# Scan and gated network on one core: ten pairs' B and C turned by a transposing DMA instead of by TensorE and VectorE

## The chip, the core and the metric

The kernel runs on one core of a Trainium2 chip. Its engines run side by side, each through its own list of instructions in the listed order: TensorE (PE in the profile; PEld for its weight loads), VectorE (DVE), ScalarE (ACT), GpSimd (POOL), and SyncE (SP), which only issues transfers. An instruction waits on semaphores for what other engines or transfers give it, and everything listed behind it on that engine waits too. Transfers run on 16 DMA engines; SP's and ScalarE's are put on hardware queues, GpSimd's on a software queue. The metric is device time in microseconds, a median over runs.

## The reference

A scan over chunks (batch 4, 8 heads, 768 tokens, head size 32, state size 16) feeds a gated network (3072 tokens, 256 to 1536 to 256).

```
cum  = cumsum(log(clip(a, 1e-6, 1)))            # within a chunk of 32 tokens
M    = (C_i . B_j) * exp(cum_i - cum_j), j <= i
y    = M @ x + exp(cum_i) * (C_i . state)
state = exp(sum) * state + sum_j exp(cum_end - cum_j) B_j x_j
...
x2   = y as (tokens, heads * head size)
out  = (max(x2 @ w_gate, 0) * (x2 @ w_val)) @ w_out
```

Inputs and output are float32.

## The kernel before, in words

**Scan.** Instead of chunks of 32 tokens the kernel uses tiles of 128 tokens with all 8 heads, two tiles to a *pair*: 12 pairs of 256 tokens, three to a batch. The decay is moved into the factors: with P the running product of a, B is scaled by 1/P and C by P, so C_i . B_j of the scaled values already holds exp(cum_i - cum_j). `cp` holds P; the matmuls `dec` and `wdec` spread it over tokens by partition, and `scaleBC` (from `dec`) or `wf` (from `wdec`) hold P and 1/P. For pair p:

- `load`, `load_wide`, `load_seq`: raw x, B, C from memory, on SP's queue.
- `scale_bc` on GpSimd multiplies B and C by their factors and rounds them to bf16; `cast_x` rounds x.
- B and C must then be turned: tokens on partitions become heads times state on partitions. `turn` does this on PE (matmuls `tp`, `tpc` against the identity), and `tevac` evacuates to `CT` and to `BT`, the latter twice with a mask `tmask`, so that of a 32-row group only one head's 16 rows are not zero.
- `G`: 16 small matmuls of BT and CT into four PSUM banks; `gevac` applies the causal mask on VectorE (`maskUT`) or copies on ScalarE and masks on GpSimd (`causal`), into `gs`.
- `astep` and `sevac` carry the state of a batch's earlier tiles (`A_ps`, `Sm`); `inter` multiplies it by CT, `Dm` multiplies gs by x; both add into the PSUM bank `y`, which `yevac` copies to `yT`.

Three forms stand in the kernel before. Pairs 0 to 3 (p < `NWIDE`) are loaded in two-token runs, so a partition holds two neighbouring tokens; the pair must be sorted back for the state, which the matmuls `bp` against `order` do (`sort_b`). Pairs 4 and 5 are loaded in token order. Batches 2 and 3 (pairs 6 to 11, p >= `NRUN`) read B and C a second time as sequences (`load_seq`), compute decays a second time in that layout (`seq_scan` to `seq_inverse`), scale them on GpSimd (`seq_scale`), turn them with 32 by 32 transposes on VectorE (`seq_turn`) and mask them there (`seq_part`); their carried state comes from `arun`, which runs the small matmuls of one or two earlier tiles into `XY`, with the masks `smasks`.

**Network.** Tokens go in 6 blocks of 512. `gv` (all 512 tokens, one slice of 128 of the 1536) and `gvp` (256 tokens, two slices) make gate and value on PE, ReLU on ScalarE, product on VectorE into `h`; `outs` multiplies h by `wo`, evacuates and stores.

**Order.** The program is one list written by hand: the last part of the function calls these pieces in the order in which each engine is to run them, so that the network's matmuls of earlier blocks stand between a pair's steps. `in_order` makes each engine keep that order. A `hold` argument puts a one-element write on VectorE ahead of a load, so that the load is issued no sooner than VectorE gets there. Weights are loaded by GpSimd's queue (`weights`, `weights_out`).

## Time and profile before

| what | value |
|---|---|
| median of 3 runs | 124.62 us (124.45 to 124.63) |
| profiled execution | 124.8 us, of it 123.0 span |
| granted TensorE clock | 1.0 |
| GpSimd busy | 40% of the span |
| read from memory, written | 11.94 MB, 3.15 MB |

The span is the time from the first to the last instruction of the program; the execution's time has 1.8 us around it. In timeline rows the first number is the start and the second the length, in microseconds from the span's start. In groups, after xcount come busy time, mean ns of one, and the idle time before them with what ended it. A DMA view names the queues (q1 is SP's, q10 ScalarE's, q0 GpSimd's) with packets, megabytes and their share of the 16 engines' time; its issue rows end with the microseconds from issue to landing. A matmul's length includes its way through the array, so starts, not lengths, show how densely PE runs.

### The profile page before, as it was taken

Reading aid. Unit: us, or ns where it says so; the run is one execution under the profiler, and the core shown is the slowest. Engines: PE = TensorE matmul, PEld = TensorE weight load, DVE = VectorE, ACT = ScalarE, POOL = GpSimd, SP = SyncE. Lnnn points to the kernel's source line nnn. Section 1 sums busy time; section 2 is a strip of 40 time slices with the busy share of each in tenths; the row PEclk is TensorE's granted clock in tenths of the full one; section 3 lists DMA queues with packets and bytes.
Section 4 is the critical chain, followed back from the end, with each engine's and each line's share of the span. In section 5 each row is a group of like instructions: output and inputs, shape, how many; then the busy total and the mean of one; then the engine's idle time right before and its main releaser. Section 6 shows DMA issues by size and latency. Waiting matters only on the chain.

```text
span 123.0 us, 3313 instructions
## 1 busy us (share of the span) xinstructions
PE 118.3 (96%) x1251; PEld 81.1 (66%) x1257; DVE 92.1 (75%) x196; ACT 74.6 (61%) x148; POOL 49.7 (40%) x102
## 2 busy tenths in 40 slices
PE   6999999999999999999999999999999999999990
PEld 4678795578888989744478644588544587444780
DVE  2786898889999859879995889981898770678420
ACT  4376668888764461767663776746676644767310
POOL 7989741885745676477330640030700030000000
PEclk9999999999999999999999999999999999999999
DMA  2999999999989979969921282003200003100022
GB/s 61 201 193 209 168 167 190 130 102 174 162 101 278 140 137 191 199 201 211 132 24 62 83 137 22 5 0 106 70 3 0 0 5 128 43 0 0 0 91 85
DMA packets 63568, 12.95 MB, mean 105 GB/s; under 512 B 55168, under 2 KB 63552, under 8 KB 63552
## 3 DMA queue, kind: packets, MB, share of 16 engines
q1 hardware_dynamic: 54160, 9.47, 42.9%
q0 software_dynamic: 4272, 2.36, 14.6%
q10 hardware_dynamic: 5120, 0.90, 3.9%
q8 instruction: 10, 0.16, 0.5%
q14 instruction: 6, 0.05, 0.1%
HBM read 11.94 MB, written 3.15 MB: 123 GB/s over the span
## 4 chain that ended last, share of the span: by engine, by line
PE 95%; DVE 1%; issue 0%; ACTq 0%; ACT 0%; DVEq 0%
PE o L760 25%; PE val L707 20%; PE gate L704 18%; PE gate L734 7%; PE val L734 6%; PE w L189 4%; PE y L670 3%; PE g L544 3%; PE y L660 2%; PE A_ps L586 1%; PE tp L486 1%; PE wdec L232 1%; PE dec L279 1%; PE o L796 1%; PE bp L463 1%; PE fdec L247 0%
## 5 line engine op out<-in xcount | busy, mean ns | idle before, releaser
L719 DVE TENSOR_TENSOR h<-r,val 128x512 bf16<-128x512 bf16 x54 | 35.9, 685 | 10.2 <-ACT r L715 9.6
L715 ACT ACTIVATE r<-gate 128x512 bf16<-128x512 f32 x54 | 32.2, 598 | 12.2 <-PE gate L704 11.7
L707 PE MATMUL val<-yT,wv 128*128 128x512 bf16 x108 | 32.1, 379 | 0.3
L760 PE MATMUL o<-wo,h 128*128 128x256 bf16 x276 | 32.3, 273 | 0.0
L704 PE MATMUL gate<-yT,wg 128*128 128x512 bf16 x102 | 30.8, 379 | 0.0
L552 POOL TENSOR_SCALAR_AFFINE_SELECT gs<-gs 128x512 bf16<-128x512 bf16 (+1 forms) x26 | 13.6, 547 | 41.6 <-ACT gs L569 41.6
L760 PEld LDWEIGHTS <-h 128*128 128x128 bf16 x276 | 26.2, 98 | 4.0
L576 DVE TENSOR_TENSOR gs<-g,maskUT 128x512 bf16<-128x512 f32 (+1 forms) x32 | 17.6, 601 | 7.1 <-PE g L544 4.0
L707 PEld LDWEIGHTS <-wv 128*128 128x128 bf16 x108 | 10.6, 98 | 12.7
L704 PEld LDWEIGHTS <-wg 128*128 128x128 bf16 x108 | 10.4, 98 | 11.1
L569 ACT CAST gs<-g 128x512 bf16<-128x512 f32 (+1 forms) x26 | 11.8, 512 | 2.9 <-PE g L544 2.9
L742 ACT ACTIVATE r<-gate 128x512 bf16<-128x512 f32 x18 | 10.6, 604 | 2.7 <-PE gate L734 2.3
L749 DVE TENSOR_TENSOR h<-r,val 128x512 bf16<-128x512 bf16 x18 | 11.8, 678 | 0.3 <-ACT r L742 0.2
L734 PE MATMUL gate<-yT,wg 128*128 128x256 bf16 x72 | 10.8, 273 | 0.0
L734 PE MATMUL val<-yT,wv 128*128 128x256 bf16 x72 | 10.8, 273 | 0.0
L779 ACT COPY ob<-o 128x512 f32<-128x512 f32 x6 | 3.5, 586 | 8.6 <-PE o L760 8.6
L774 ACT COPY ob<-o 128x256 f32<-128x256 f32 x10 | 3.7, 373 | 7.3 <-PE o L760 6.8
L734 PEld LDWEIGHTS <-wv 128*128 128x128 bf16 x72 | 7.0, 98 | 0.9
L692 ACT CAST yT<-y 128x512 bf16<-128x512 f32 x10 | 5.9, 586 | 2.4 <-PE y L670 2.3
L734 PEld LDWEIGHTS <-wg 128*128 128x128 bf16 x72 | 6.7, 98 | 0.9
L189 PE MATMUL w<-warm 128*128 128x256 bf16 x27 | 5.9, 380 | 1.2 <-DVE tmask L159 1.2
L452 POOL CAST xb<-xr 128x512 bf16<-128x512 f32 x10 | 6.1, 612 | 1.0 <-DMA xr<-in_x_dram 1.0
(124 smaller groups left out, 123.2 us busy)
## 6 DMA issues: line engine op xcount, KB each, us to landing
xr<-in_x_dram SPq DMA_DIRECT2D x24, 128.0 KB, 3.7
out_dram<-ob SPq DMA_DIRECT2D x6, 256.0 KB, 2.6
out_dram<-ob SPq DMA_DIRECT2D x9, 128.0 KB, 1.8
wo<-in_moe_w_out_dram POOLq DMA_DIRECT2D x1, 768.0 KB, 8.9
seqB<-in_B_dram SPq DMA_DIRECT2D x2, 384.0 KB, 3.7
seqC<-in_C_dram SPq DMA_DIRECT2D x2, 384.0 KB, 4.2
br<-in_B_dram SPq DMA_DIRECT2D x12, 64.0 KB, 3.2
wg<-in_moe_w_gate_dram POOLq DMA_DIRECT2D x3, 128.0 KB, 4.3
```

What stands on the lines that cost most here:

```text
L189: nc.tensor.matmul(out=w[:, 0:cols], lhsT=warm[:, 0:128], rhs=warm[:, 0:cols], start=True, stop=True)
L552: nc.gpsimd.affine_select(out=dst, in_=dst, pattern=[[0, n], [1, 128]], compare_op=ALU.is_ge, fill=0.0, base=0, channel_multiplier=-1)
L569: nc.scalar.copy(out=d[:, q, h], in_=g[q][:, h])
L576: nc.vector.tensor_tensor(out=d[:, q, h], in0=g[q][:, h], in1=m[:, h], op=ALU.mult)
L704: nc.tensor.matmul(out=g, lhsT=wg[:, k, fs], rhs=yT[:, k, tk], start=(k == 0), stop=(k == 1))
L707: nc.tensor.matmul(out=v, lhsT=wv[:, k, fs], rhs=yT[:, k, tk], start=(k == 0), stop=(k == 1))
L715: nc.scalar.activation(r, g, AF.Relu)
L719: nc.vector.tensor_tensor(out=fst[b][:, f], in0=r, in1=v, op=ALU.mult)
L734: nc.tensor.matmul(out=o[:, j], lhsT=w[:, k, fs], rhs=yT[:, k, tk], start=(k == 0), stop=(k == 1), skip_group_check=True)
L742: nc.scalar.activation(r, g, AF.Relu)
L749: nc.vector.tensor_tensor(out=fst[b][:, f:f + 2, u * 256:(u + 1) * 256], in0=r, in1=v, op=ALU.mult)
L760: nc.tensor.matmul(out=o[:, ts % 2], lhsT=fst[b][:, f, ts * 128:(ts + 1) * 128], rhs=wo[:, f], start=(f == 0), stop=(f == NF - 1), skip_gr ...
```

## The change

Pairs 0 and 1 stay as they are (`NWIDE` is 2). Pairs 2 to 11 all take one form:

- `load_bc` loads C in two-token runs (`cr`) and B in token order (`br`, two loads of 64 KB).
- The decays come from `dec` alone: `decay_evac` copies them on ScalarE, in two parts, to `cN`; `inverse` makes `iN` = 1/cN on VectorE; `decay_sort` brings cN into two-token order, `wC`, by four transfers on SP's queue, from SBUF to SBUF.
- `scale_bc` on GpSimd writes B, scaled by iN, into the diagonal blocks (`diag`) of one of four tiles `pads` whose rest was set to zero once: for each of the two token tiles one slice with the even heads and one with the odd ones, 128 columns each. C, scaled by wC, goes into two more slices. For pairs 6 to 11 a fourth multiply writes B without padding, for `arun`.
- `dturn` turns the six slices with one transposing DMA on SP's queue into `TT` (128 x 6 x 128, bf16). G reads TT: the zeros of the padding take the place of the masked second copy of BT.
- The state step of pairs 2 to 5 uses the padded slices: two matmuls of 128 columns, even and odd heads, in place of one of 256; no sorting matmuls.
- C's two-token order makes the columns of G, gs and y run over the even, then the odd tokens: the causal masks have that order (`maskW`, a longer pattern in `causal`), and `yevac` writes every other column of yT.
- The second decays, sequence loads, scalings, turns and masks of batches 2 and 3 go, and so do `turn`, `sort_b`, `tevac` and `wdec` for pairs 2 to 5.
- x of pair 1 is loaded behind the first scaling multiply of pair 0 on VectorE; the holds on pair 3's loads go; B and C of pair 3 are loaded ahead of x of pair 2.

On SP, from the start of its list to the loads of pair 3's x. Before (xr is raw x, bcr raw B and C):

```order
L138 DMA a_sb<-in_a_dram 64x384
L95 DMA xr<-in_x_dram 128x8x32 x4
L83 DMA bcr<-in_B_dram 128x8x32
L83 DMA bcr<-in_C_dram 128x8x32
L95 DMA xr<-in_x_dram 128x8x32 x2
L83 DMA bcr<-in_B_dram 128x8x32
L83 DMA bcr<-in_C_dram 128x8x32
L95 DMA xr<-in_x_dram 128x8x32 x2
```

and now:

```order
L119 DMA a_sb<-in_a_dram 64x384
L95 DMA xr<-in_x_dram 128x8x32 x4
L105 DMA cr<-in_C_dram 128x8x32
L109 DMA br<-in_B_dram 128x8x16 x2
L288 DMA wC<-cN 64x80 x4
L105 DMA cr<-in_C_dram 128x8x32
L109 DMA br<-in_B_dram 128x8x16 x2
L95 DMA xr<-in_x_dram 128x8x32 x2
L342 DMA_TRANSPOSE TT<-pad_119 128x6x128
L342 DMA_TRANSPOSE TT<-pad_120 128x6x128
L95 DMA xr<-in_x_dram 128x8x32 x2
```

The transposes of pairs 2 and 3 stand behind the loads of B and C of both pairs and x of pair 2, and the loads of pair 3's x behind the transposes.

On GpSimd, from pair 1's last weights to the load of wo. Before (bs is a pair's scaled B and C, xb rounded x):

```order
L202 DMA wv<-in_moe_w_val_dram 128x2x384
L433 TENSOR_TENSOR bs<-bcr,wf_437 128x512
L452 CAST xb<-xr 128x512
L552 AFFINE_SELECT gs<-gs 128x512 x2
L552 AFFINE_SELECT gs<-gs 128x256
L433 TENSOR_TENSOR bs<-bcr,wf_437 128x512
L206 DMA wo<-in_moe_w_out_dram 128x12x256
```

and now:

```order
L189 DMA wv<-in_moe_w_val_dram 128x2x384
L315 TENSOR_TENSOR pad_119<-br,iN 128x4x2x16 x2
L319 TENSOR_TENSOR pad_119<-cr,wC 128x256
L315 TENSOR_TENSOR pad_120<-br,iN 128x4x2x16 x2
L319 TENSOR_TENSOR pad_120<-cr,wC 128x256
L367 CAST xb<-xr 128x512
L835 MEMSET pad_117 128x512
L835 MEMSET pad_118 128x512
L449 AFFINE_SELECT gs<-gs 128x512 x2
L449 AFFINE_SELECT gs<-gs 128x256
L193 DMA wo<-in_moe_w_out_dram 128x12x256
```

Both pairs are scaled, two tiles cleared and pair 2's x rounded ahead of pair 2's masks and the load of wo.

On PE, ahead of G of pair 2, between groups 6 and 7 of block 0. Before (bs is scaled B and C, ident the identity):

```order
L707 MATMUL val<-yT,wv 128x512
L486 LDWEIGHTS bs
L486 MATMUL tp<-ident,bs 128x128
L486 LDWEIGHTS bs
L486 MATMUL tp<-ident,bs 128x128
L486 LDWEIGHTS bs
L486 MATMUL tpc<-ident,bs 128x128
L486 LDWEIGHTS bs
L486 MATMUL tpc<-ident,bs 128x128
L463 LDWEIGHTS order
L463 MATMUL bp<-bs,order 128x128
```

and now, at the end of group 7:

```order
L620 MATMUL val<-yT,wv 128x512
L620 LDWEIGHTS wv
L620 MATMUL val<-yT,wv 128x512
L438 LDWEIGHTS TT
L438 MATMUL g_527<-TT 128x128
```

Group 7 follows group 6 without the transposes and sorting matmuls, and G reads TT.

The core of the diff:

```diff
-    NWIDE = 4
+    NWIDE = 2
...
+    def load_bc(p, q=nc.sync, hold=False):
+        br = raw.tile([128, 2, NH, N], FP32, tag="br", name="br")
+        cr = raw.tile([128, NH, 2, N], FP32, tag="cr", name="cr")
+        if hold:
+            nc.vector.memset(cr[0:1, 0, 0, 0:1], 0.0)
+        sl = slice(c0 * 128, (c0 + 2) * 128)
+        q.dma_start(out=cr.rearrange("p h r n -> p h (r n)"),
+                    in_=C[b, :, sl, :].rearrange("h (p r) n -> p h (r n)", r=2))
         for i in range(2):
             sl = slice((c0 + i) * 128, (c0 + i + 1) * 128)
+            q.dma_start(out=br[:, i], in_=B[b, :, sl, :].rearrange("h s n -> s h n"))
...
+    def decay_evac(d, part):
+        by = cN.rearrange("p i (b t) h -> p i t b h", t=PPB)
+        if not part:
+            nc.scalar.copy(out=by[:, 0, 0:2], in_=d[:, 0:HC:2, 0])
+            nc.scalar.copy(out=by[:, 1, 1:3], in_=d[:, 0:HC:2, 1])
+        else:
+            nc.scalar.copy(out=by[:, 1, 0], in_=d[:, 1, 0])
+            nc.scalar.copy(out=by[:, 0, 2], in_=d[:, 1, 1])
+    def decay_sort():
+        for i in range(2):
+            for r in range(2):
+                nc.sync.dma_start(out=wC[64 * i:64 * i + 64, r, NWIDE:NPAIR],
+                                  in_=cN[r:128:2, i, NWIDE:NPAIR])
+    def inverse(p0, p1):
+        nc.vector.reciprocal(iN[:, :, p0:p1], cN[:, :, p0:p1])
...
+        if p >= NWIDE:
+            s["pad"] = t = pads[p % NPAD]
+            for i in range(2):
                 eng.tensor_tensor(
+                    out=diag(t, 2 * i), in0=s["br"][:, i].rearrange("s (q t) n -> s q t n", t=2),
+                    in1=iN[:, i, p].rearrange("s (q t) -> s q t", t=2).to_broadcast(
+                        [128, 4, 2, N]), op=ALU.mult)
+            eng.tensor_tensor(
+                out=t[:, 4:6].rearrange("s r (h n) -> s r h n", n=N),
+                in0=s["cr"].rearrange("s h r n -> s r h n"),
+                in1=wC[:, :, p].to_broadcast([128, 2, NH, N]), op=ALU.mult)
...
+    def dturn(p):
+        s = st[p]
+        s["TT"] = att.tile([128, 6, 128], BF16, tag="TT", name="TT")
+        nc.sync.dma_start_transpose(out=s["TT"], in_=s["pad"].rearrange("s k m -> s (k m)"))
...
     first_scale(0, fB, bs0[:, 0:2])
+    load_x(1, True)
     first_scale(1, dC, bs0[:, 2:4])
...
-    load_wide(2, nc.sync, True)
-    load_x(2)
+    load_bc(2, nc.sync, True)
...
-    decay_evac(dall)
+    decay_evac(dall, 0)
     split_y(0)
+    decay_evac(dall, 1)
+    decay_sort()
+    load_bc(3)
+    load_x(2)
...
-    d2 = wide_decay([2, 3], later)
-    wide_factors([2, 3], d2)
     gvp_mul(*u4)
-    load_wide(3, nc.sync, True)
+    scale_bc(2, nc.gpsimd)
+    dturn(2)
+    scale_bc(3, nc.gpsimd)
+    dturn(3)
     load_x(3)
...
-    u = gv_relu(*gv(0, 6, False))
-    turn(2, True)
-    sort_b(2, False)
-    tevac(2, nc.vector, nc.scalar)
-    gv_mul(*u)
-    sort_evac(2)
+    gv(0, 6)
     gv(0, 7)
     G(2)
...
+        if more:
+            scale(Q, nc.gpsimd, nc.gpsimd)
+        if P + 3 < NPAIR:
+            load(P + 3)
+        if more:
+            dturn(Q)
+        if P + 4 < NPAIR:
+            load(P + 4)
...
             if f == 4 and R < NPAIR:
                 scale(R, nc.gpsimd, nc.gpsimd)
+                dturn(R)
```

350 lines of the change are left out of this document (101 added, 249 removed).

## The prediction

> **What bounds the kernel now.** I read the page first: engines, slices, chain of waits.
>
> ```profile
> span 123.0 us, 3313 instructions
> PE 118.3 (96%) x1251; PEld 81.1 (66%) x1257; DVE 92.1 (75%) x196; ACT 74.6 (61%) x148; POOL 49.7 (40%) x102
> DMA  2999999999989979969921282003200003100022
> PE 95%; DVE 1%; issue 0%; ACTq 0%; ACT 0%; DVEq 0%
> ```
>
> TensorE (PE) is busy for 96% of the span and makes 95% of the chain. A microsecond off PE's list is a microsecond off the time; one off VectorE, ScalarE or GpSimd is worth nothing by itself. The DMA engines are the second resource: a slice is 3.1 us, and from the second slice to about 58 us they are nearly full. A step that comes to hang on a DMA in that stretch waits behind a backlog.
>
> **What leaves PE's list.** The timeline of PE around the operations that go:
>
> ```profile
> 15.13 0.27 PE L586 MATMUL A_ps<-xb,bx 128*128 128x256 bf16 x1
> 15.33 0.68 PE L232 MATMUL wdec<-pick,cp 64*64 64x8 f32 x16
> 15.94 0.61 PE L734 MATMUL gate<-yT,wg 128*128 128x256 bf16 x4
> ...
> 19.43 0.28 PE L486 MATMUL tp<-ident,bs 128*128 128x128 bf16 x2
> 19.55 0.28 PE L486 MATMUL tpc<-ident,bs 128*128 128x128 bf16 x2
> 19.66 0.39 PE L463 MATMUL bp<-bs,order 128*128 128x128 bf16 x4
> 19.88 0.59 PE L704 MATMUL gate<-yT,wg 128*128 128x512 bf16 x2
> ...
> 20.84 0.40 PE L544 MATMUL g<-CT,BT 32*128 32x128 bf16 x16
> ...
> 22.05 0.27 PE L586 MATMUL A_ps<-xb,bx 128*128 128x256 bf16 x1
> 22.16 0.59 PE L704 MATMUL gate<-yT,wg 128*128 128x512 bf16 x2
> ...
> 36.79 0.39 PE L486 MATMUL tp<-ident,bs 128*128 128x128 bf16 x4
> 37.01 0.60 PE L734 MATMUL gate<-yT,wg 128*128 128x256 bf16 x4
> ```
>
> On a pipelined engine, start to start tells what an operation holds. The 16 decay matmuls of pairs 2 and 3 hold 15.94 - 15.13, less 0.11 for the A_ps matmul (22.05 to 22.16): 0.70. The four transposes and four sorting matmuls of pair 2 hold 19.43 to 19.88: 0.45. Pair 3 has the same eight: 0.45. The four transposes of pair 4 hold 36.79 to 37.01: 0.22, and pair 5's as much. Sum **-2.04 us**. What PE gains: six state steps become two matmuls of 128 columns in place of one of 256; two such hold 0.12 (19.43 to 19.55) against 0.11, so nothing. From pair 6 on PE's list keeps its length.
>
> If nothing else changed, the profiled execution of 124.8 (123.0 of span, 1.8 around it) would become 122.8; against the median of 124.62, which is 0.2 under that execution, 122.6.
>
> **What PE then waits for.** G(2) got its operands from PE by way of VectorE and ScalarE. Now it waits for a longer chain: ScalarE's copies of the decays, four small transfers into wC, GpSimd's three multiplies, the transposing DMA (T2). G(2) would be reached at 20.84 - 0.70 - 0.45 = 19.69. The question is when T2 lands. It stands on SP's queue behind the loads of x for pairs 0 to 2 and of B and C for pairs 2 and 3. SP's timeline before; then the packets of SP's queue (q1) in the DMA view of the windows 3:6, 9:12, 12:15, 15:18, 18:21 and 21:24; last the landing time of the x load that starts at 20.28:
>
> ```profile
> 17.25 0.37 SPq L83 DMA_DIRECT2D bcr<-in_B_dram  x1
> 20.28 0.58 SPq L95 DMA_DIRECT2D xr<-in_x_dram  x1
> ...
> q1 hardware_dynamic: 2080, 0.26, 56.0%
> q1 hardware_dynamic: 2309, 0.29, 67.7%
> q1 hardware_dynamic: 1590, 0.20, 47.6%
> q1 hardware_dynamic: 1669, 0.21, 52.2%
> q1 hardware_dynamic: 2702, 0.34, 73.1%
> q1 hardware_dynamic: 3260, 0.40, 88.1%
> ...
> xr<-in_x_dram SPq DMA_DIRECT2D x1, 128.0 KB, 3.3
> ```
>
> A load of x or wide C is 1,024 rows of 128 bytes, half a pair's B is 1,024 rows of 64. Ahead of T2 stand four loads of x for pairs 0 and 1, three for pair 2's B and C, three for pair 3's, two of x(2): 12 x 1,024 = 12,288 rows, and 4 x 64 into wC. Before, exactly 12 such loads stand up to the x load of 20.28, and it landed at 20.28 + 3.3 = 23.6. So as many rows as landed at 23.6 must go before T2, and it comes sooner only as far as the queue starts sooner. It does twice. First, x(1): its marker on VectorE moves from 7.13 to behind the first scaling multiply, at about 5.6.
>
> ```profile
> 5.24 0.42 DVE L261 TENSOR_TENSOR bs<-bcr,wf 128x256 bf16<-128x256 f32 x1
> 7.13 0.06 DVE L92 MEMSET xr<- 1x1 f32 x1
> ```
>
> Second, the hold on pair 3's B and C until 17.25 goes away. I take the queue as moving from 7.0 without a break. By 6.0 it had done 2,080, which leaves 12,288 + 256 - 2,080 = 10,464. Beside the weights it ran 2309 / 3 = 770 a us: 13.6 us, so 20.6. T2 itself is 128 x 6 pieces of 256 bytes; at the 1,087 a us of the last window 0.7. From a last packet to its landing: through the x load of 20.28 the queue had 12,288 packets, 10,350 of them by 21.0 (the sum of the first five rows), so the last 1,938 were through at about 22.8 and landed 0.8 later. T2 lands at 20.6 + 0.7 + 0.8 = **22.1**, G(2) begins at 22.2, and PE stands for 22.2 - 19.69 = **2.5 us**. PE works in its listed order, so the four remaining gate and value groups of block 0 stand behind G(2) and cannot fill the gap.
>
> The bounds. No backlog: the rows from SBUF say what a transfer of 192 KB takes alone, between 1.8 and 2.6.
>
> ```profile
> out_dram<-ob SPq DMA_DIRECT2D x6, 256.0 KB, 2.6
> out_dram<-ob SPq DMA_DIRECT2D x9, 128.0 KB, 1.8
> 15.08 0.72 POOL L202 DMA_DIRECT2D wv<-in_moe_w_val_dram  x1
> L419 POOL TENSOR_TENSOR bt<-br,scaleBC 128x128 bf16<-128x128 f32 x12 | 4.6, 405 | 0.0
> ```
>
> GpSimd is free at 15.8; two multiplies of 0.405 and one of twice that size end at 17.4 if wC is there; plus 2.2 is 19.6, no wait at all, and the whole -2.04 stays. Other side: no gain from the earlier start, T2 at 23.6 + 0.7 = 24.3, a wait of 4.7 and a net of +2.7. My value lies between, nearer the backlog, because the DMA row is at 9 in those slices.
>
> By the Trainium skill, Advanced Engine Details and Errata, section X-Bar Transpose (TRN2), transposing DMAs are as fast as ordinary ones, 350 to 400 GB/s; T2's 192 KB would then be an estimated 0.5 us in place of 0.7, and the sum 0.2 lower. No run here shows one yet.
>
> **The rest.** T3 is issued right behind T2, and between G(2) and G(3) PE has the rest of block 0's gate and value groups, pair 2's products and two groups of block 1: covered. The weights wo are issued behind pair 2's masks on GpSimd, 1.4 later than before, as G(2) is (22.2 - 20.84):
>
> ```profile
> 24.53 1.07 POOL L206 DMA_DIRECT2D wo<-in_moe_w_out_dram  x1
> 37.89 1.47 PE L760 MATMUL o<-wo,h 128*128 128x256 bf16 x12
> wo<-in_moe_w_out_dram POOLq DMA_DIRECT2D x1, 768.0 KB, 8.9
> ```
>
> 25.9 + 8.9 = 34.8, against a first use at 37.89 - 1.82 (what is saved by then) + 2.5 = 38.6: covered by 3.8, and T4, which queues behind that traffic, by some 1 to 2. Pair 6 is tighter: its T stands on SP behind the first output of block 0 (41.87) and the five loads of pair 7.
>
> ```profile
> 41.87 0.39 SPq L780 DMA_DIRECT2D out_dram<-ob  x1
> 44.94 0.58 SPq L106 DMA_DIRECT2D br<-in_B_dram  x1
> 49.74 0.40 PE L544 MATMUL g<-CTs,BM 32*128 32x128 bf16 x16
> br<-in_B_dram SPq DMA_DIRECT2D x12, 64.0 KB, 3.2
> ```
>
> Four loads were landed at 44.94 + 3.2 = 48.1, 6.3 after the output; a fifth (0.9) and T6 (0.7) make 7.9, and G(6) comes 49.74 - 41.87 - 0.22 = 7.65 after it: **+0.2**, between 0 and 0.8. Later transposes have over 3 us, in slices where the DMA row stands at 0 to 3. ScalarE's two extra copies, the reciprocals, GpSimd's longer scaling (0.405 x 4 = 1.6 a pair) and the two-token mask and copy patterns lie on engines with 25 to 60% idle: 0 unless they sit between G(2) and its users. VectorE and ScalarE lose the evacuations of the transposes and the second decays: 0.
>
> Sum: -2.04 + 2.5 + 0.2 = **+0.7**: 125.5 for such an execution, 125.3 as a median.
>
> **Rivals.** *T2 in time.* It lands before 21.2, the wait is 0 to 1.6 and the net -2.0 to -0.2: 122.6 to 124.4. For it: the hold on pair 3, 2 us of SP's queue by itself, is gone, and T2 is small. Against: 12,288 rows ahead of it. It ends where wait and saving cancel, at a landing of 21.4 (21.5 - 19.69 - 2.04 + 0.2 = 0). Chance 0.30.
>
> *Transposes that hold the queue.* If one takes some 3 us in place of 0.7, T2 lands past 24.4; SP stands meanwhile, so x(3) and pair 4 run into wo, and T4 comes after G(4). From the upper bound's +2.7 on: 127.3 to 129. For it: no transpose by DMA stands in this trace. Against: it moves 768 pieces, fewer than one load of x. Chance 0.12.
>
> *A cold PE.* The same 256-column matmul at the start and later:
>
> ```profile
> 1.16 3.17 PE L189 MATMUL w<-warm 128*128 128x256 bf16 x14 [1.16 <-DVE tmask L159]
> 7.70 0.71 PE L189 MATMUL w<-warm 128*128 128x256 bf16 x5
> ```
>
> 3.17 / 14 is 0.21 each against 0.11: PE ran the first microseconds at half rate. If a long stand brings that back for 3.4 us, it costs 1.7 on top: 127. The Trainium skill, TensorE: Matmul & The Clock Gate, Part 1, has PE fall to half clock after a whole idle window of 3.4 us that runs free; by that rule a stand of 2.5 costs nothing more. Chance 0.06.
>
> **How the numbers follow.** Forecast, a stand at G(2) that outweighs the saving or cancels it, 0.52; T2 in time 0.30; the other two 0.18. From no change the measurement tells about 0.2%, 0.25 us. Of the forecast's 0.52, 0.13 falls within it (T2 at 21.2 to 21.7): same 0.13, slower 0.39 + 0.18 = 0.57, faster 0.30. The likeliest case alone spans 124.4 to 126.6 (T2 at 21.2 to 23.4). The range takes in most of the early case and the first half of the late ones: 123.0 to 127.5.
>
> **What would show it.** Right: in PE's timeline a gap of 2 to 3 us before the first G on TT, put down to the transposing DMA, with wdec gone and the gate and value groups back to back from 15.2; no gap at G(3). Wrong: no gap there and an end 2 us earlier (T2 was fast or not behind the loads); T2 landing after 24; PE rows at 0.21 after the gap; a gap at G(4) or G(6) larger than 1 us.

## The result: 5.6% slower

The changed kernel takes 131.53 us (median of 5 executions, 130.75 to 132.11) where the kernel before takes 124.46 beside it: a ratio of 1.0562, with a 95% interval of 1.0515 to 1.0608. The profiled execution took 131.21, its span 129.5. The forecast was 125.3, the range 123.0 to 127.5. The sign was right, the size was not: 7 us instead of 0.7. (Here and below a median is of all executions, and a ratio leaves the few disturbed ones out.)

The page of the changed kernel (span; PE's busy time; PE in slices; the granted clock in slices; the chain that ended last):

```profile
span 129.5 us, 3218 instructions
PE 118.8 (92%) x1217; PEld 79.7 (62%) x1223; DVE 82.0 (63%) x158; ACT 74.1 (57%) x144; POOL 49.7 (38%) x100
PE   6999891598989999999999999999999999999990
PEclk9999999559999999999999999999999999999998
PE 79%; DMA 10%; ACT 4%; SPq 2%; issue 1%; DVE 1%; ACTq 0%
```

PE has 34 matmuls less and yet is busy for 0.5 us more. The chain has 10% of DMA and 4% of ScalarE, which were not in it before. In PE's row the slice with a 1 (19.4 to 22.7) and half of the next are a stand; in the row of the clock two slices show 5 (22.7 to 29.1): half rate. Nearly all that was lost lies in the seventh to the twelfth slice.

PE's timeline there:

```profile
15.41 0.60 PE L647 MATMUL gate<-yT,wg 128*128 128x256 bf16 x4 [0.35 <-ACT yT L561]
...
19.32 0.59 PE L620 MATMUL val<-yT,wv 128*128 128x512 bf16 x2
24.23 0.61 PE L438 MATMUL g<-TT 32*128 32x128 bf16 x16 [4.31 <-DMA TT<-pad]
25.60 1.06 PE L620 MATMUL val<-yT,wv 128*128 128x512 bf16 x2
...
31.29 0.38 PE L617 MATMUL gate<-yT,wg 128*128 128x512 bf16 x1 [0.51 <-ACT yT L605]
...
33.78 0.40 PE L438 MATMUL g<-TT 32*128 32x128 bf16 x16
...
38.30 0.49 PE L647 MATMUL gate<-yT,wg 128*128 128x256 bf16 x3 [0.51 <-ACT yT L605]
```

The last two val matmuls ahead of G(2) were through at 19.32 + 2 x 0.216 = 19.75; the forecast had PE there at 19.69. Then PE stood for T2 until 24.23: 4.48 us. The gate and value pairs behind it take 1.06 where the same pair took 0.59 at 19.32: half clock. And three gate matmuls wait for ScalarE's copies into yT, which nothing did before: at 15.41 for pair 1's, at 31.29 and 38.30 for those of pairs 2 and 3. From one G to the next the two profiles compare like this (us):

| stretch | before | after | difference | made of |
|---|---|---|---|---|
| start to PE's arrival at G(2) | 20.84 | 19.75 | -1.09 | pair 2's turn and sort 0.45, an earlier start 0.35, the later decays 0.18, 0.11 spread |
| the stand at G(2) | 0 | 4.48 | +4.48 | T2 |
| G(2) to G(3) | 6.86 | 9.55 | +2.69 | half clock 2.46, wait on yT 0.68, less pair 3's turn and sort 0.45 |
| G(3) to G(4) | 11.70 | 12.04 | +0.34 | wait on yT 0.67, less 0.33 (pair 4's turn) |
| G(4) to G(5) | 5.27 | 5.05 | -0.22 | pair 5's turn |
| G(5) to G(6) | 5.07 | 5.27 | +0.20 | wait for T6 |
| G(6) to the end | 73.26 | 73.36 | +0.10 | |

The sum is 6.5, the difference of the spans. (The 2.46 is what is left of 2.69 when the other two are taken off; the first experiment measures it.)

Where T2 spent its time shows in SP's timeline (start, duration and what SP issued):

```profile
12.64 3.24 SPq L288 DMA_DIRECT2D wC<-cN  x4
15.93 0.59 SPq L105 DMA_DIRECT2D cr<-in_C_dram  x1
16.57 2.42 SPq L109 DMA_DIRECT2D br<-in_B_dram  x2
19.03 1.21 SPq L95 DMA_DIRECT2D xr<-in_x_dram  x2
20.33 2.95 SPq L342 DMA_TRANSPOSE TT<-pad  x2
```

in GpSimd's, at the multiply for C:

```profile
19.24 0.62 POOL L319 TENSOR_TENSOR pad<-cr,wC 128x256 bf16<-128x256 f32 x1 [2.01 <-DMA wC<-cN]
```

and in the packets of SP's queue (q1), in the window 6:21 and in 15:18:

```profile
q1 hardware_dynamic: 9171, 0.94, 49.8%
...
q1 hardware_dynamic: 930, 0.10, 25.4%
```

Pair 2's second load of x, the last thing ahead of T2, landed at 23.45, T2 at 24.18. The pad was ready at 19.86. The queue moved 9,171 packets from 6 to 21 us, where the forecast had taken 770 a us from 7.0 on, 10,780 by then; in 15:18 it moved 930. The multiply for C waited for the last of the four transfers into wC, which landed at 19.09.

### The profile page after: what moved, and what is told of

The parts are those of the page before. It is cut to its first block, busy times and chain, and to the rows that moved or that the text cites. A ratio compares the mean times of both kernels' runs of the same rounds, so it can differ in the third digit from the quotient of the medians.

```text
span 129.5 us, 3218 instructions
## 1 busy us (share of the span) xinstructions
PE 118.8 (92%) x1217; PEld 79.7 (62%) x1223; DVE 82.0 (63%) x158; ACT 74.1 (57%) x144; POOL 49.7 (38%) x100
## 4 chain that ended last, share of the span: by engine, by line
PE 79%; DMA 10%; ACT 4%; SPq 2%; issue 1%; DVE 1%; ACTq 0%
PE o L673 20%; PE val L620 18%; PE gate L617 18%; DMA TT<-pad 6%; PE gate L647 5%; PE val L647 4%; PE w L176 4%; PE g L438 3%; DMA br<-in_B_dram 2%; PE y L580 2%; SPq L288 2%; ACT yT L605 1%; DMA out_dram<-ob 1%; ACT gs L466 1%; PE y L570 1%
## 5 line engine op out<-in xcount | busy, mean ns | idle before, releaser
L632 DVE TENSOR_TENSOR h<-r,val 128x512 bf16<-128x512 bf16 x54 | 37.0, 687 | 15.7 <-ACT r L628 15.3
L628 ACT ACTIVATE r<-gate 128x512 bf16<-128x512 f32 x54 | 32.3, 598 | 15.0 <-PE gate L617 13.4
L620 PE MATMUL val<-yT,wv 128*128 128x512 bf16 x107 | 32.9, 389 | 0.3
L617 PE MATMUL gate<-yT,wg 128*128 128x512 bf16 x103 | 32.6, 394 | 0.5 <-ACT yT L605 0.5
L449 POOL TENSOR_SCALAR_AFFINE_SELECT gs<-gs 128x512 bf16<-128x512 bf16 (+1 forms) x26 | 14.1, 566 | 46.6 <-ACT gs L466 46.6
L473 DVE TENSOR_TENSOR gs<-g,maskW 128x512 bf16<-128x512 f32 (+1 forms) x28 | 15.0, 588 | 12.8 <-issue 12.2
L620 PEld LDWEIGHTS <-wv 128*128 128x128 bf16 x108 | 10.9, 101 | 14.4 <-issue 2.4
L662 DVE TENSOR_TENSOR h<-r,val 128x512 bf16<-128x512 bf16 x18 | 11.9, 680 | 2.0 <-ACT r L655 1.8
L605 ACT CAST yT<-y 128x512 bf16<-128x512 f32 x10 | 7.3, 734 | 2.5 <-PE y L580 2.4
L500 DVE TENSOR_TENSOR Sm<-A_ps,smask 128x256 bf16<-128x256 f32 x10 | 4.2, 418 | 7.2 <-PE A_ps L488 7.2
L315 POOL TENSOR_TENSOR pad<-br,iN 128x128 bf16<-128x128 f32 x20 | 7.8, 403 | 1.9 <-DMA br<-in_B_dram 1.9
L438 PE MATMUL g<-TT 32*128 32x128 bf16 x160 | 4.2, 225 | 4.4 <-DMA TT<-pad 4.3
```

Of the source, the lines that this page charges most:

```text
L449: nc.gpsimd.affine_select(out=dst, in_=dst, pattern=[[0, n], [1, 2], [2, 64]] if wide else [[0, n], [1, 128]], compare_op=ALU.is_ge, fill= ...
L473: nc.vector.tensor_tensor(out=d[:, q, h], in0=g[q][:, h], in1=m[:, h], op=ALU.mult)
L605: eng.copy(out=dst, in_=src)
L617: nc.tensor.matmul(out=g, lhsT=wg[:, k, fs], rhs=yT[:, k, tk], start=(k == 0), stop=(k == 1))
L620: nc.tensor.matmul(out=v, lhsT=wv[:, k, fs], rhs=yT[:, k, tk], start=(k == 0), stop=(k == 1))
L628: nc.scalar.activation(r, g, AF.Relu)
```

## The experiments

### What the 6.5 us consist of

**e1_warm** keeps PE busy during the stand:

```
     gv(0, 7)
+    keep_warm(40)
     G(2)
```

> The changed kernel with 40 small matmuls on zeros (256 columns, about 4.3 us at full clock) in front of G(2), where PE stands idle for 4.5 us. My theory: of the 7.0 us lost, 2.5 come from the clock, which the records show at half from 22.6 to 29.4 us because PE stood idle before it. PE busy there, G(2) comes when it did (24.2, perhaps 0.2 later), the clock stays full, and the run takes 129.0 (128.6 to 129.5). Rival A, the clock falls for another reason (its load, or something at a fixed time): half clock again from about 22.6, 131.5 or a little more. Rival B, the cold clock is only a label and the slow rows come from something else in that stretch (memory traffic): the clock full, rows of 512 columns still at 0.43 us, 131.5.

Measured 130.74 us, ratio 1.0452 (1.0374 to 1.0530). PE's timeline:

```profile
25.54 0.40 PE L438 MATMUL g<-TT 32*128 32x128 bf16 x16 [1.06 <-DMA TT<-pad]
26.32 0.59 PE L620 MATMUL val<-yT,wv 128*128 128x512 bf16 x2
...
32.63 0.40 PE L438 MATMUL g<-TT 32*128 32x128 bf16 x16
```

The clock stays full, a pair takes 0.59 again, and G(2) to G(3) takes 7.09 instead of 9.55 for the same list: 2.46 us is the price of the clock, and the stand is its cause, since nothing else was changed. Rivals A and B fall. The time fell by less than expected: in this profile T2 landed 1.3 us later, at 25.50, and T8 at 73.09, so that PE waited for it at G(8). The small matmuls need not be why. Seven profiles have this order on SP (the changed kernel's, e1, e2, e8, e10, e16, e18), and T2 landed anywhere from 24.18 to 25.50 in them, at 24.91 in the median; the changed kernel's is the earliest.

**e2_yt** splits the copy into yT by its k half:

```
-            eng.copy(out=dst, in_=src)
+            for k in range(2):
+                eng.copy(out=dst[:, k], in_=src[:, k])
```

> The changed kernel with ScalarE's copy of a pair's output into yT as two copies, one for each half of the 256 model columns, from pair 2 on. My theory: the one copy with its four-dimensional pattern is taken to cover all that lies between its first and last element, so the second gate matmul of groups that read only the earlier pairs (block 0's twelfth group, block 1's eleventh and twelfth) waits for it; 0.68 us behind pair 2's products and 0.67 behind pair 3's. With two plain patterns both waits go: 130.2 (129.9 to 130.5), no wait on yT in those two places. Rival: PE would have stood there anyway, for banks or for the next groups, which do read the copied pair: the wait moves to the next group and the run takes 131.2 to 131.6.

Measured 130.52 us (130.20 to 130.87), ratio 1.0452 (1.0406 to 1.0498): 1.1% or 1.4 us under the changed kernel, about what was expected. The total is no measure of the two waits by itself: in this profile the clock was at half for 3.4 us, not 6.8, and T2 landed 0.54 later. The rows are. Neither wait is there, G(3) to G(4) takes 11.37 in place of 12.04, and the first group that had waited runs through:

```profile
29.81 0.41 PE L580 MATMUL y<-gs,xb 128*32 128x128 bf16 x16
30.15 0.61 PE L620 MATMUL gate<-yT,wg 128*128 128x512 bf16 x2
```

Both waits were on tokens that those groups never read. The change had turned a copy whose output is two plain rows of 256 into one whose output runs as (k, r, m). The waits fit a dependency on all that lies between its first and last element, which takes in the k = 1 half of earlier tokens, and two copies without such a span have none.

**e16_ytwarm** is both edits together, with no line of its own.

> The changed kernel with the copy into yT in halves and the 40 small matmuls on zeros ahead of G(2). Theory: the parts add. 131.5, less 1.35 for the waits on yT, less 2.4 for the clock: 127.8 (127.3 to 128.5), ratio 1.022 to 1.032, the clock full throughout; what is left over the time before is T2's lateness, 4.4, less what the change saves. Rival: T2 comes later when PE is busy (it landed at 25.5 with the small matmuls alone), and the gain of the clock is lost there again: 129 to 130.

Measured 130.40 us (130.09 to 131.10), ratio 1.0446 (1.0404 to 1.0488): hardly under either alone, although the clock is full and neither of the two waits on yT is left. The table of G's tells why. With T2 at 24.9, G(4) comes at 42.74, 3.1 us ahead of the changed kernel. Then 1.4 us of the lead are given back, in PE's timeline:

```profile
48.09 0.40 PE L438 MATMUL g<-TT 32*128 32x128 bf16 x16 [0.24 <-DMA TT<-pad]
...
53.72 0.40 PE L438 MATMUL g<-TT 32*128 32x128 bf16 x16 [0.48 <-DMA TT<-pad]
...
72.25 0.40 PE L438 MATMUL g<-TT 32*128 32x128 bf16 x16 [0.72 <-DMA TT<-pad]
```

T5, T6 and T8 stand on SP's queue behind loads for later pairs; as soon as PE comes earlier it waits for them. In the changed kernel itself T7 landed at 68.78 with G(7) at 68.83, T8 at 73.81 with G(8) at 73.88: no margin was left.

**e18_sum** adds to e16 the order that the fourth group of experiments found (each transposing DMA from T5 on ahead of the loads, five output buffers).

> The changed kernel with everything but the stand at G(2) mended: the copy into yT in halves, the 40 small matmuls ahead of G(2), the transposing DMAs from T5 on ahead of the loads, five output buffers. Theory: the parts add, and what e16 gained up to G(4) was given back by later transposes that came late once PE came earlier: no wait on TT behind G(2), 130.4 less 1.4 to 1.9: 128.7 (128.2 to 129.2), ratio 1.028 to 1.034. With T2 at 24.2 to 25 instead of an arrival at 19.7 that is the lateness alone, 4.5 to 5.2, less the 0.9 saved in pairs 3 to 5. Rival: the later waits are replaced by others, 130 or more.

Measured 127.79 us, ratio 1.0193 (1.0148 to 1.0237): 0.9 better than expected. No wait on TT is left but this one:

```profile
24.88 0.40 PE L438 MATMUL g<-TT 32*128 32x128 bf16 x16 [0.62 <-DMA TT<-pad]
```

(0.62 after the small matmuls, 5.1 after PE's arrival.) So of the 5.6% the clock, the copy and the places of the later transfers make 3.7 points, and what stays, 1.9%, is T2's lateness less the savings: 5.1 less the 1.09, 0.45, 0.33 and 0.22 of the table is 3.0, and the spans differ by 3.1 (126.1 and 123.0).

### Why T2 is late

**e3_nosort** takes the four small transfers away, and leaves the reordering of C's decays out of the computation.

```
-    decay_sort()
...
-                in1=wC[:, :, p].to_broadcast([128, 2, NH, N]), op=ALU.mult)
+                in1=cN[:, :, p].to_broadcast([128, 2, NH, N]), op=ALU.mult)
```

> The changed kernel without the four small transfers that bring the decays into two-token order; C is scaled by the decays in token order instead, which is another factor (that part of the computation is left out). My theory: these four hold SP's queue for 3.25 us (12.64 to 15.88), and everything behind them, T2 last, is 3.25 later for it; GpSimd's multiply for C also waits 2.0 us for them. T2 is issued at about 18.5 instead of 20.3 and lands at 21.5 to 22 instead of 24.2, the stand at G(2) is 2 us instead of 4.5, too short to lose the clock: 126.5 (126 to 127.5). Rival, the transposing DMA or the backlog of packets sets the landing, not the time of issue: T2 lands at 23.5 or later, 130 to 131.5.

Measured 130.88 us (130.19 to 131.23), ratio 1.0473 (1.0419 to 1.0528); T2 landed at 24.23. My theory falls: 3.25 us of SP's time were given free, and T2, expected at 21.5 to 22, came no sooner than in the changed kernel's profile. (Against the median of the seven, 24.91, it may have come some 0.7 sooner.) SP's timeline:

```profile
12.88 1.80 SPq L105 DMA_DIRECT2D cr<-in_C_dram  x1
14.73 2.79 SPq L109 DMA_DIRECT2D br<-in_B_dram  x2
17.56 2.97 SPq L95 DMA_DIRECT2D xr<-in_x_dram  x2
20.63 2.69 SPq L342 DMA_TRANSPOSE TT<-pad  x2
```

The issue of the same loads begins 3 us earlier, but takes SP 7.6 us instead of 4.2: it is held back while it issues, and x lands at 23.39 against 23.45. The time of issue did not set the landing. SP's queue moved 2,100 packets in 15:18 against 930, but 2,478 in 18:21 against 3,731; the last weights on GpSimd's queue landed at 20.06 against 18.91; and all queues together moved 2.54 MB from 6 to 21 us against 2.63. That fits DMA engines which the loads share with the weights and which are full; no run took the weights out of this stretch to show it.

**e4_x2late** puts x of pair 2 behind T2.

```
     load_bc(3)
-    load_x(2)
...
     dturn(2)
+    load_x(2)
```

> The changed kernel with pair 2's two loads of x behind T2 on SP's queue instead of ahead of it. My theory (first in, first out on the queue): T2 is issued at 19.9, when the pad is ready, and lands at about 22.3, 1.9 earlier; PE stands 2.5 us at G(2) and keeps its clock. x of pair 2 then lands 1.5 to 2 us later than now, at about 25, is cast by 26 and the state step behind G(2) waits up to 2 us for it. In all 127 to 129. Rival, T2 takes its 3.9 us whatever stands ahead of it: T2 lands at 23.8, the stand stays over 4, and the state step waits on top: 131 to 133.

Measured 130.66 us, ratio 1.0455 (1.0404 to 1.0506). T2 was issued at 19.73, when the pad was ready, and landed at 23.47: 0.7 earlier, not 1.9, and earlier than in any of the seven profiles. It took 3.7 us from its issue on, with 2,048 packets less ahead of it: the rival's mechanism, though the time lies between the two.

**e5_plain** is e4 with ordinary copies in place of the transposing DMAs, so that B and C are not turned.

```
-        nc.sync.dma_start_transpose(out=s["TT"], in_=s["pad"].rearrange("s k m -> s (k m)"))
+        nc.sync.dma_start(out=s["TT"].rearrange("s k m -> s (k m)"),
+                          in_=s["pad"].rearrange("s k m -> s (k m)"))
```

> The kernel with pair 2's x behind T2, and every transposing DMA replaced by an ordinary one that copies the pad into TT row by row (128 rows of 1,536 bytes); the transposition is left out, so what the products read is not turned. With x out of the way T2 still took 3.7 us from its issue (19.7) to its landing (23.5). Theory A, the transposing is what takes that long: the copy is issued at 19.7 as before and lands as an output of this size does, 2.2 us later (1.8 for 128 KB, 2.6 for 256 KB), at about 22, the stand at G(2) is 2 us and the clock stays full; x of pair 2 is still late, so the time is 128.5 to 129.5 against 130.7 there. Theory B, the backlog of the queue takes that long: the copy lands at 23 or later and the time stays at 130.3 to 130.9.

Measured 129.36 us, ratio 1.0262 (1.0185 to 1.0338). Two of the four executions kept the clock (128.10 and 128.26; the ratio is theirs), two had a mean granted clock of 0.974 and 0.973 and took 130.54 and 130.45. The profile is of one that kept it. The copy was issued at 19.48 and landed at 21.89, 2.4 us later: theory A. PE's timeline shows what came in its place:

```profile
21.94 0.40 PE L439 MATMUL g<-TT 32*128 32x128 bf16 x16 [1.81 <-DMA TT<-pad]
...
24.82 0.27 PE L489 MATMUL A_ps<-xb,pad 128*128 128x128 bf16 x2 [1.50 <-POOL xb L368]
```

PE now waits for x of pair 2, which stands behind T2. Over all ten transposes the price is smaller; these are the rows by transfer of the changed kernel, and then of e5 (the last number is the median from issue to landing; in e4 it is 3.3):

```profile
TT<-pad SPq DMA_TRANSPOSE x10, 3.2
```

```profile
TT<-pad SPq DMA_DIRECT2D x10, 192.0 KB, 2.7
```

**e11_early** is e3 and e4 together: no small transfers, x behind T2.

> The changed kernel without the four small transfers (C scaled by another factor: that part of the computation is left out) and with x of pair 2 behind T2: both of the two things that alone brought T2 no further than 24.2 and 23.5. Theory A: each alone only uncovered the other, T2 was held by the loads of x on the queue and by the decays on GpSimd at once; with both gone the pad is ready at 18.5 to 19.0 and T2 lands 3.7 us later, 22.2 to 22.7. PE stands 2.5 to 3 at G(2), the state step behind it waits up to 0.5 for x; with the clock kept 127.3 to 128.3, with the clock lost 129 to 130. Theory B: B and C of pair 3 (2,048 rows more) and the weights on the other queue fill the engines until 21, T2 lands at 23.3 or later whatever is issued when, and the time is 130.2 or more.

Measured 130.76 us, ratio 1.0460 (1.0404 to 1.0516). Both theories are half right. T2 was issued at 18.56 and landed at 21.67, earlier than theory A had it. PE did not stand for it in this profile, but partly because it was late itself: its clock rose to full only at 9.81 (at 5.49 in the changed kernel's), and it came to G(2) some 1.6 us later. The time is theory B's:

```profile
21.72 0.40 PE L438 MATMUL g<-TT 32*128 32x128 bf16 x16 [0.22 <-ACT r L628]
...
25.86 0.27 PE L488 MATMUL A_ps<-xb,pad 128*128 128x128 bf16 x2 [2.77 <-POOL xb L367]
```

x of pair 2 landed at 25.08, and the stand had only moved to the state step, half clock behind it and all. Pair 2 needs both T2 and x, and whichever was last on the queue landed between 23.2 (T2 in e13) and 26.7 (x in e12) in every order that was tried.

**e13_bc3late** leaves both, and moves pair 3's B and C from ahead of them to behind T2 (on top of e2).

```
-    load_bc(3)
     load_x(2)
...
     dturn(2)
+    load_bc(3)
+    load_x(3)
```

> The changed kernel with the copy into yT in halves, and pair 3's loads of B and C moved on SP's queue from ahead of pair 2's x to behind T2 (GpSimd's scaling of pair 3 behind pair 2's masks, T3 after that). Theory A, the order on the queue is the cause: 2,048 rows less stand ahead, x of pair 2 lands by 21, T2 is issued at 19.9, when the pad is ready, and lands at 22.7 to 23.2; nothing else waits at G(2) or behind it, T3 lands at 29 and G(3) comes at 29.5. From the 130.5 of that kernel without the move 1.7 less, 128.8, and 126.3 in executions that keep the clock. Theory B, the sum of rows in the first 24 us is the cause: pair 3's loads come too late instead, PE stands 1.5 us or more at G(3), and the time stays at 130 or more.

Measured 132.86 us, ratio 1.0647 (1.0575 to 1.0719): no better than the change itself, theory B. (Its executions took 131.46, 131.94, 133.78 and 134.30; the interval overlaps the change's, so that it is worse is not shown.) PE's timeline:

```profile
23.26 0.61 PE L438 MATMUL g<-TT 32*128 32x128 bf16 x16 [3.12 <-DMA TT<-pad]
...
34.22 0.40 PE L438 MATMUL g<-TT 32*128 32x128 bf16 x16 [1.63 <-DMA TT<-pad]
```

and the times from issue to landing in the window 26:36:

```profile
wo<-in_moe_w_out_dram POOLq DMA_DIRECT2D x1, 768.0 KB, 8.9
...
TT<-pad SPq DMA_TRANSPOSE x1, 6.6
```

x of pair 2 landed at 20.70, but T2 still took 3.7 us and landed at 23.22; T3, now issued at 27.6 beside the load of wo (27.5), took 6.6 us and was late at G(3). No order of these transfers that was tried helped: T2, x of pair 2, or T3, one of them is late. All were on SP's queue; no run put the transposes on another. **e15_bc3fill**, which added the move of the next paragraph, gave 131.6 to 134.1 us without a ratio, and tells nothing beyond it.

> The same with block 0's ninth and tenth gate and value groups ahead of G(2). Theory A: PE reaches G(2) at 21.6 and stands 1.1 to 1.6 us, the clock stays full; behind G(2) PE waits some 0.6 for pair 2's masks, as with this move before. 126.3 less 1.74 plus 0.6: 125.2 (124.8 to 125.8), the same as before within 1%. Theory B: with 1.74 less cover T3 and x of pair 3 are late by that much more, and the time is 127.5 or more.

### Work into the stand

**e8_fill** was to move block 0's ninth and tenth groups ahead of G(2). The edit left them in the old place too, so that they were computed twice:

```
     gv(0, 7)
+    gv(0, 8)
+    gv(0, 9)
     G(2)
-    u = gv(0, 8, False)
+    u = gv(0, 10, False)
```

> The changed kernel with the copies into yT in two halves, and with block 0's ninth and tenth gate and value groups ahead of G(2) in place of behind it (1.74 us of PE's work that needs nothing of pair 2). My theory: T2 lands at 24.2 to 24.7 as before, but PE stands 2.8 us instead of 4.5 and keeps its clock: 130.5 less 1.74 less 1.7 to 2.5 is 126.3 to 127.1. Rival: the groups were the cover of pair 2's masks behind G(2), and of ScalarE's copy; without them PE stands in front of pair 2's products for as long, and only the clock is won: 128 to 128.8.

130.44 us, ratio 1.0417 (1.0322 to 1.0511). With the double work it tells only that PE, arriving 1.74 later, still stood 3.4 us. **e10_fill2** has them once.

> What e8_fill was meant to be: there the two groups moved ahead of G(2) were left in their old place too and were computed twice; now they stand only ahead of G(2). In e8_fill PE stood 3.4 us and lost its clock in three runs of four; that stand stays. Theory: what is gone is two groups behind G(2), 1.74 us at full clock and up to 3.4 at half: 130.4 less that, 127.3 to 128.7, in the runs that keep the clock 1.5 less. Rival: the two groups covered ScalarE's copies and the masks of pair 2; PE stands over 1 us in front of pair 2's products, and the time is 129 or more.

Measured 130.44 us, ratio 1.0411 (1.0336 to 1.0485): a miss, the rival's time. One execution kept the clock and took 128.91; three had a mean granted clock of 0.972 to 0.974 and took 130.34, 130.53 and 130.88. The profile is of such a one: T2 landed at 25.12, PE stood 3.36 us, the clock was half from 26.0 to 32.8 (in e2 from 25.3 to 28.7), and 0.6 us of new waits for pair 2's state and masks came behind G(2). The 1.74 us moved into the stand were paid back by a second window of 3.4 us at half clock.

**e12_all** put e2, e4, this move and the later order together.

> The changed kernel, whole, with all that helped: the copy into yT in halves, two groups ahead of G(2), x of pair 2 behind T2, each transposing DMA ahead of the loads. Theory: the losses add up. From 131.5: the waits on yT 1.35, T2 0.7 earlier, 1.74 of work moved into the stand, 2.5 for the clock that stays full when PE stands under 2.2 us, T6 0.2, less 0.7 for x of pair 2, which comes late: 125.7 (125.2 to 126.5), and 127 to 128 in runs that lose the clock all the same. Rival: the pieces overlap (what stands in the gap is needed behind it), 127.5 or more with the clock full.

Measured 131.58 us, ratio 1.0528 (1.0457 to 1.0599): the rival. PE's timeline:

```profile
23.09 0.40 PE L438 MATMUL g<-TT 32*128 32x128 bf16 x16 [1.37 <-DMA TT<-pad]
...
27.53 0.37 PE L488 MATMUL A_ps<-xb,pad 128*128 128x128 bf16 x2 [3.07 <-POOL xb L367]
```

What filled the stand at G(2) was missing in the wait for x that follows.

### What transposing DMAs are worth in pairs 4 to 11

**e6_four** leaves pairs 2 and 3 as they were before.

```
-    NWIDE = 2
+    NWIDE = 4
```

(and the lines for pairs 2 and 3 as in the kernel before: two-token loads, decays, turn, sort and evacuations on PE, VectorE and ScalarE.)

> The changed kernel with pairs 2 and 3 handled as in the kernel before (two-token loads, their own decays on PE, transposes and sort on PE) and pairs 4 to 11 by transposing DMA. My theory: all that was lost lies at G(2) and behind it, from pairs 2 and 3 alone; pairs 4 and 5 save their 0.44 us of transposes, pair 6 pays 0.2, the rest is even: 124.2 (123.9 to 124.6), 0.3% under before, no wait on TT over 0.4 us anywhere. Rival: the transposing DMAs also cost in the later pairs (other engines' traffic, longer scaling on GpSimd, the strided copies): 125.3 or more.

Measured 126.13 us, ratio 1.0080 (1.0042 to 1.0119). So 4.8 of the 5.6% lie in pairs 2 and 3, but the 0.3% of gain is not there. The profile is of the longest execution, 129.93, whose clock rose to full only at 17.05; PE was 4.4 us later at G(2) than in e14 (25.10 and 20.67), so its waits are a hint and no measure. PE stands there for T6 and T8:

```profile
53.98 0.40 PE L438 MATMUL g<-TT 32*128 32x128 bf16 x16 [0.46 <-DMA TT<-pad]
...
72.40 0.40 PE L438 MATMUL g<-TT 32*128 32x128 bf16 x16 [0.63 <-DMA TT<-pad]
```

**e7_three** has pair 2 as before and pair 3 by DMA (with the split copy):

```
-    NWIDE = 2
+    NWIDE = 3
...
+    scale(2, nc.gpsimd, nc.gpsimd)
+    scale_bc(3, nc.gpsimd)
+    dturn(3)
```

> Pair 2 as in the kernel before, pairs 3 to 11 by transposing DMA, T3 issued behind x of pair 3 and B and C of pair 4, and the copy into yT in two halves for those pairs. My theory: a transposing DMA is harmless where its operands have been there for long and G is some microseconds off. PE loses the eight transposes and sorts of pair 3 (0.45), the eight of pairs 4 and 5 (0.44) and half of the later decays (up to 0.35): 123.5 (123.1 to 123.9). T3 is issued at 22 to 23 and lands at 26, G(3) stands at about 26.5. Rival, any transposing DMA in the first 30 us comes late by the queue's backlog: T3 lands at 27.5 or later, PE stands 1 us or more at G(3), 124.5 or more.

Measured 129.08 us, ratio 1.0318 (1.0265 to 1.0370): worse, and not for either reason. PE's timeline, and GpSimd's:

```profile
26.26 0.23 PE L580 MATMUL y<-gs,xb 128*32 128x128 bf16 x2 [2.43 <-POOL gs L449]
```

```profile
23.71 0.40 POOL L315 TENSOR_TENSOR pad<-br,iN 128x128 bf16<-128x128 f32 x1 [1.50 <-DMA br<-in_B_dram]
```

My edit had put pair 3's scaling ahead of pair 2's masks on GpSimd; the scaling waited for pair 3's B until 23.7, the masks for the scaling, and PE for the masks, with half clock after it. It is the same kind of loss in another place: work queued behind a wait. T3 itself landed at 28.18, and G(3) came at 31.35 without a wait for it.

**e9_order** is e6 with T6, T7 and T8 ahead of the loads on SP.

```
-    load(7)
     scale_bc(6, nc.gpsimd)
     dturn(6)
+    load(7)
...
+        if more:
+            dturn(Q)
         if P + 3 < NPAIR:
             load(P + 3)
-        if more:
-            dturn(Q)
-        if P + 4 < NPAIR:
-            load(P + 4)
...
                 dturn(R)
+                if P + 4 < NPAIR:
+                    load(P + 4)
```

> Pairs 2 and 3 as in the kernel before and pairs 4 to 11 by transposing DMA, and now each transposing DMA ahead of the loads on SP's queue: T6 ahead of pair 7's loads, T7 ahead of pair 9's, T8 ahead of pair 10's. Without that order this kernel took 1.008 of the time before (I had expected 0.997), with PE standing 0.46 us at G(6) and 0.63 at G(8) for TT. Theory A, these waits are what was missing: transposes issued when their pad is ready land 1 to 3 us before they are needed, and the time is 124.7 (124.3 to 125.1), ratio 0.998 to 1.002, no wait on TT at all. Theory B, the rest of the loss lies in the first 20 us (the four small transfers and the decays' copies delay the loads): the waits go, but 125.4 or more, ratio 1.004 or more.

Measured 125.50 us, ratio 1.0031 (1.0004 to 1.0059), between the two theories. Those waits are gone, and one at G(5) has come:

```profile
45.61 0.40 PE L438 MATMUL g<-TT 32*128 32x128 bf16 x16 [1.48 <-DMA TT<-pad]
```

**e14_four2** puts x of pair 6 behind T5 as well.

```
     load_x(5)
-    load(6)
+    load_bc(6)
...
     dturn(5)
+    load_x(6)
```

> Pairs 2 and 3 as in the kernel before, pairs 4 to 11 by transposing DMA, each of these ahead of the loads, and now T5 also ahead of pair 6's x (two loads, some 1.3 us of SP's queue). Theory A: T5 lands 1.3 us earlier and the wait of 1.48 at G(5) falls under 0.3; the transposes of pairs 4 and 5 show as a gain at last: 124.4 (124.0 to 124.8), ratio 0.993 to 0.999. Theory B: the wait at G(5) was one execution's, the rest is even and what is lost lies at the beginning (other order of loads): ratio 1.000 to 1.006 again.

Measured 124.46 us (before: 124.62), ratio 0.9977 (0.9953 to 1.0001): theory A. No wait on TT is left. One of another kind is, on PE, and behind it on ScalarE:

```profile
53.67 0.59 PE L620 MATMUL val<-yT,wv 128*128 128x512 bf16 x2 [0.68 <-ACT ob L687]
```

```profile
53.25 0.37 ACT L687 COPY ob<-o 128x256 f32<-128x256 f32 x1 [2.69 <-DMA out_dram<-ob]
```

An output transfer stood on SP's queue behind the loads and kept its buffer.

**e17_four3** gives the outputs five buffers in place of three.

```
-        ob = ffn.tile([128, 2, DM], FP32, tag="ob", name="ob", bufs=3)
+        ob = ffn.tile([128, 2, DM], FP32, tag="ob", name="ob", bufs=5)
```

> Pairs 2 and 3 as in the kernel before, pairs 4 to 11 by transposing DMA ahead of the loads, and five output buffers in place of three. Theory: the outputs of block 0 and 1 stand on SP's queue behind transposes and loads, an output buffer was free only at 53.2, ScalarE's copy waited for it and the relu and PE behind that, 0.68 us; with five buffers the wait is gone: 123.9 (123.5 to 124.3), ratio 0.992 to 0.996. Rival: the wait was in that one profile, or goes elsewhere: 0.996 to 1.000 as it was.

Measured 124.39 us (before: 124.86), ratio 0.9961 (0.9933 to 0.9990): 0.4% under the kernel before, with 94% of its chain on PE. In its profile the wait on ob at 53.67 is gone. That the buffers gave the last 0.2% is not shown, since the interval overlaps that of e14.

## Why the prediction was wrong, step by step

**What leaves PE's list.** Right: PE reached G(2) at 19.75 (forecast 19.69), and pairs 2 to 5 gave 0.45, 0.45, 0.33 and 0.22 against 0.45, 0.45, 0.22 and 0.22. One item was wrong: the decay matmuls of pairs 2 and 3, put at 0.70, gave 0.18. Behind them stood a wait for ScalarE's copy of pair 1 into yT (the row at 15.41), which they had covered. An earlier start of 0.35, which I had not counted, made up most of that; that PE's arrival came out within 0.06 of the forecast is luck.

**When T2 lands.** This step failed: 22.1 was forecast, 24.2 measured, a stand of 4.48 in place of 2.5. Its structure held: T2 was behind 12,288 rows and the small transfers, and it landed 0.73 after the last of them (forecast 0.7). The term that was mis-sized is the pace of the queue, 770 packets a us without a break from 7.0. The rows ahead of T2 landed 2.05 us later than that gives (23.45 against 21.4): with the same 0.8 to landing, 10,464 rows in 15.6 us, 670 a us. I had read the pace in the best of the three windows from 9 to 18 us, beside the weights, and did not hold it against the other two rows of the same fence, 1,590 and 1,669 in 3 us. The "other side" bound, no gain from the earlier start, 24.3, was what happened. e3 shows that taking the small transfers away brings little there. A second term would have failed behind the first. The pad was ready at 19.86, because wC landed at 19.09, and my chain gave it no time of its own outside the bound with no backlog, 17.4; and from its issue on T2 takes 2.8 to 3.7 us in that traffic even with x or pair 3's loads behind it (e12, e11, e4, e13), so that a T2 issued at 19.86 lands at 22.7 or later. Only e11, with the small transfers gone and x behind T2, brought a transposing T2 under the 22.1 of the forecast.

**A cold PE.** Named, with a chance of 0.06 and a price of 1.7; it came, at 2.46: the half clock lasted not one window of 3.4 us but two (22.56 to 29.39), and PE worked through 5.2 us of them. e1 shows that the stand is the cause. (The half rate itself was read a little low: 3.17 / 14 is 0.23, not 0.21.) The condition was wrong as well: I had let a stand under 3.4 us go free. In e12 the clock fell after a window of 3.41 us that had 1.37 us of matmuls in it (last section). The Trainium skill, TensorE: Matmul & The Clock Gate, Part 1, has the clock fall after a whole idle window; the runs here don't agree with "idle" taken as no work at all.

**The rest at 0.** Wrong in one item: the pattern of the copy into yT, listed among things that lie on idle engines, cost 1.35 through waits on a tile, not through ScalarE's time, as e2 shows.

**T6 and the later transposes.** T6's +0.2 was right (0.20). "Later transposes have over 3 us" was wrong: T7 and T8 landed 0.05 and 0.07 before their G. It cost nothing in the changed kernel, since PE was late itself, but it took back 1.4 us in e16 and, as e9 and e14 show, the whole gain in e6. I had looked at how idle the engines are there, not at what stands on SP's queue ahead of each transpose.

**The rivals.** Transposes that hold the queue for 3 us, given 0.12, came closest: one takes SP 1.27 us and lands after 3.2 at the median, a plain copy 2.7. But none held the queue for 3 us: T3 landed 0.63 after T2. The Trainium skill, Advanced Engine Details and Errata, section X-Bar Transpose (TRN2), has the two as equally fast; by the landings that is off by 0.5 us. The estimate of 0.5 us from its bandwidth was of the moving alone.

## What to carry to other kernels

Before work is moved from a busy engine to a queue of transfers, read the pace of that queue in every window up to the moment of need and take the slowest, and add the transfer's own time from issue to landing: in the busy stretch here an earlier issue moved little, and one transfer put ahead made another late. A stall on the bound engine has a second price, the clock behind it, and a wait that is removed often uncovers the next, so that fixes have to be counted together (here 2.5 and 1.4 us gave 0.1 more than either alone until the later transposes were put ahead of the loads). The gain, 0.4%, was there in the pairs whose operands lie ready long before, and only with each transfer placed ahead of the prefetches that can wait.

## What the runs showed of the hardware

**The clock does not need an idle window to fall.** The changes of the granted clock lie 3.41 us or a multiple of it apart within a profile. These are the windows so cut, from the changed kernel, from e7, from e12 and from e5, which kept the clock (window, its length, then PE, PEld, DVE, ACT and POOL busy, clock, share of DMA, GB/s):

```profile
19.15:22.56 3.41, 0.76 (x4) 0.15 (x2) 1.38 (x2) 0.70 (x2) 2.01 (x4) 1.00 1.14 147
22.56:25.97 3.41, 1.74 (x19) 0.78 (x20) 0.00 (x0) 1.04 (x3) 1.92 (x4) 0.50 0.93 153
25.97:29.39 3.42, 3.42 (x11) 1.42 (x10) 2.48 (x5) 1.40 (x4) 2.92 (x5) 0.50 0.83 96
```

```profile
26.48:29.89 3.41, 2.83 (x22) 1.50 (x22) 0.44 (x1) 1.18 (x2) 2.34 (x4) 0.50 0.95 145
```

```profile
21.80:25.21 3.41, 1.37 (x20) 0.64 (x21) 0.69 (x1) 1.76 (x5) 0.46 (x1) 1.00 1.37 159
...
28.62:32.04 3.42, 2.83 (x23) 1.20 (x22) 1.26 (x3) 1.35 (x3) 3.04 (x5) 0.50 1.05 132
```

```profile
19.02:22.44 3.42, 1.61 (x23) 0.64 (x21) 1.68 (x3) 1.07 (x3) 1.76 (x4) 1.00 1.00 163
```

Windows with 0.76 and 1.37 us of matmuls (0.36 to 1.37 over eleven profiles, up to 1.38 at the ends of the programs) ended in half clock. The emptiest full-clock windows that did not had 1.49 (e9, from 119.38), 1.61 (e5) and 1.67 (e15, from 21.93). So in these runs the limit lies between 1.38 and 1.49 us of matmuls in 3.41: some 2 us of stand in one window are enough, and where the windows lie decides whether the fall comes. At half clock a window with 3.42 brought full rate back in the changed kernel; with 2.83 one did (e7, full from 29.89) and one did not (e12, full only from 35.46). At the start of e6 windows with 3.33, 3.41 and 3.41 did not either (full from 17.05), so what brings it back is more than the time of matmuls and stays open.

**SP is held back while it issues.** A load of 1,024 rows takes SP 0.4 to 0.6 us to issue at the least, and up to 1.8 us between 9 and 20 us in the changed kernel; in e3, where the loads were issued earlier, up to 2.3; and 3.7 once, at 32.3, beside the load of wo. What limits it (the queue's length, the traffic of the weights beside it) was not separated.
